# Packed attention and feed-forward on one core: the second-stage matrix P is produced already turned

## The chip, the cores and the metric

The kernel runs on one core of one Trainium2 chip. The metric is device time in microseconds (us) of one execution; lower is better. Engines are named as the profile names them: PE is TensorE's matmul stream, PEld its stream of weight loads, DVE VectorE, ACT ScalarE, POOL GpSimd, SP SyncE (it issues most of the DMAs).

## The reference, cut to what matters

```python
batch, n_heads, seq, head_dim = (8, 8, 576, 64);  n_pack = 32
n_tokens, d_model, d_ff = (4608, 512, 2048)

def sm_attn(qq, kk, vv):
    s = scale * np.matmul(qq, kk.transpose(0, 1, 3, 2))
    s = s - np.max(s, axis=-1, keepdims=True)
    a = np.exp(s)
    a = a / (np.sum(a, axis=-1, keepdims=True) + 1e-09)
    return np.matmul(a, vv)
p_packed = sm_attn(p, k, v)                # 32 packed rows per head: "P"
out = sm_attn(q, p_packed, p_packed)
x = out.transpose(0, 2, 1, 3).reshape(4608, 512)
h = x @ w_in
g = h * (1.0 / (1.0 + np.exp(-1.702 * h)))
return g @ w_out
```

Everything is fp32 outside. The sum of the first softmax runs over the 576 keys; P has, for each of 8 heads, 32 rows of 64 numbers.

## The kernel before, in words

The batches are numbered 0 to 7. Each goes through these steps, one function for each. `scores1` makes the first scores on PE, `scores1_copy` brings them out, `scores1_max` and `bias1` find the maxima, `exp1` takes the exponentials on ACT and adds up their rows, and `sum1` makes half the reciprocal of each sum (`rs1`), a scalar for each of 128 partitions. A partition of these tiles is one packed row of one of four heads; there are two such tiles of 128x576 for a batch, counted by `eo` (0 for even heads, 1 for odd ones). `turn1_blocks` turns 32x32 blocks on DVE, `turn1_out` and `turn1_in` send the blocks through DRAM and back, four stores for each tile and six loads for the batch, and so the weights lie with keys on partitions in `aT`: five groups of 128 keys (`c`), two parities (`e`), 128 columns.

`pack` multiplies them with v. It makes 5 x 2 x 4 = 40 small matmuls, in order of `c`, `e` and the head pair `j`: the stationary side is 128 keys x 32 columns of `aT`, the moving side 128 keys x 64 columns of v, and the four `j` write four strips of 32 partitions. Its result is P, packed rows on partitions, in two PSUM banks (6 and 7). `pack_end` copies the two halves out on ACT, scaled by `rs1`; `pack_turn_mm` turns the 128x128 tile on PE; and `pack_turn_copy` copies the turned tile (`pt`) into SBUF.

`scores2_mm` multiplies `pt` with q into the bank pair `hh`, `scores2_turn` to `turn2` are the second softmax (DVE, POOL, ACT), and `a_upper` / `a_lower` split its weights into two rounded parts. `m_chunk` multiplies `pt` with w_in into M. Then `hp_mm` multiplies M with the second weights (12 matmuls of 288 columns, a pair of feed-forward chunks) into `hh`; `hp_tanh` (ACT) and `hp_gate` (DVE) take the result out of `hh`, which has no second buffer, so `hp_mm` of one pair and `scores2_mm` wait for `hp_gate` of the pair before. `sums_1` to `sums_3`, `g_upper` and `g_lower` prepare its output, and `product` (three matmuls of 256 columns) or `plain` (three of 512) multiply it with w_out into four accumulators `acc`. `take_1` to `take_6` combine those into output rows, `keep` and `keep_over` store them.

The order of all the work is one tuple of 3546 steps, written out by hand or by a planner outside; each engine works through its own instructions in that order, strictly one after the other, and waits are set where data or a buffer ask for it. Steps of attention for one batch stand between the feed-forward steps of the batch ahead of it. Batch 0 goes its own way (`pack_first`, `pack_first_half`, `pack_first_end`), which is the same in both kernels.

Lines of the profile: L184 `warm`, L372 `scores1`, L444 `exp1`, L521 `pack`, L566 `pack_end`, L572 `pack_turn_mm`, L593 `m_chunk`, L627 `scores2_mm`, L635 `scores2_turn`, L702 the gate, L709 `hp_mm`, L759 `out_mm` (the second product of batch 0), L815 `hp_tanh`, L875 `product` and `plain`, L899 to L923 the takes, L934 `keep_over`; L178 and L180 are the copy helper on ACT and on another engine.

Of the kernel before, what the change touches and what calls it, by code (L numbers as in the profile page):

```python
# [24 lines left out]
def kernel(  # L25
# [116 lines left out]
    def bank(i):  # L142
        return pair[0][:, i - 4, :] if pair and i in (4, 5) else banks_all[i]
# [366 lines left out]
    def pn_tile():  # L510
        return words(PN, P).rearrange("p (e d) -> p e d", d=D)

    def pack(b, banks):
        vt = kq["v", b]
        st["bank", "P", b] = [bank(i) for i in banks]
        for c in range(KC):
            for e in range(2):
                t = st["bank", "P", b][e]
                for j in range(NP):
                    e0 = (2 * j + e) * D  # L520
                    nc.tensor.matmul(  # L521
                        t[32 * j : 32 * j + 32, e * D : (e + 1) * D],
                        aT[:, c, e, 32 * j : 32 * j + 32], vt[c][:, e0 : e0 + D],
                        start=(c == 0), stop=(c == KC - 1),
                    )
# [29 lines left out]
    def pack_first_end(b):  # L555
        for eo in range(2):
            t = st["bank", "Pf", 1, eo]
            nc.vector.scalar_tensor_tensor(
                pn_tile()[:, eo, :], t[:, eo * D : (eo + 1) * D], rs1(eo), pf[:, eo, :],
                op0=ALU.mult, op1=ALU.add,  # L560
            )

    def pack_end(b):
        for eo in range(2):
            t = st["bank", "P", b][eo]
            nc.scalar.activation(  # L566
                pn_tile()[:, eo, :], t[:, eo * D : (eo + 1) * D], AF.Copy, scale=rs1(eo)
            )
# [362 lines left out]
    def keep_over(n, i, k, engine=nc.sync):  # L931
# [43 lines left out]
        (m_chunk, 0, 0, (6, 7), 1), (load, 'v', 1, 1), (join_w, 5), (m_upper, 0, 0, 0, 1, act),  # L975
        (h_mm, 0, 1, 1, 5), (m_upper, 0, 0, 1, 1, dve), (upper_w, 5, act), (m_lower, 0, 0, 0, 1),
        (out_mm, 0, 0, 3), (h_tanh, 0, 1, 1), (m_lower, 0, 0, 1, 1), (lower_w, 5, pool),
        (begin_w, 9), (h_gate, 0, 1, 1), (h_mm, 0, 2, 0, 4), (begin_w, 6), (h_mm, 0, 2, 1, 5),
        (join_w, 9), (h_upper, 0, 1, 1, act), (join_w, 6), (h_tanh, 0, 2, 0), (out_mm, 0, 1, 0),
        (begin_w, 7), (h_lower, 0, 1, 1, pool), (out_mm, 0, 1, 1), (h_over, 0, 0, dve),  # L980
        (h_gate, 0, 2, 0), (h_tanh, 0, 2, 1), (h_over, 0, 1, dve), (join_w, 7), (begin_w, 8),
        (h_mm, 0, 3, 1, 4), (over_out, 0), (h_gate, 0, 2, 1), (load, 'v', 1, 0), (begin_w, 11),
        (out_mm, 0, 0, 2), (join_w, 8), (load_w, 13), (begin_w, 10), (out_mm, 0, 1, 2),
        (h_over, 0, 2, dve), (join_w, 11), (load_w, 12), (upper_w, 6, act), (h_mm, 0, 3, 0, 5),
        (join_w, 10), (upper_w, 7, act), (lower_w, 6, pool), (scores1_max, 1, 1),
        (m_chunk, 0, 1, (6, 7), None), (h_tanh, 0, 3, 1), (h_upper, 0, 2, 1, act), (bias1, 1, 1),
        (h_gate, 0, 3, 1), (h_upper, 0, 2, 0, act), (h_lower, 0, 2, 1, pool),
        (m_upper, 0, 1, 1, None, act), (m_upper, 0, 1, 0, None, dve), (out_mm, 0, 1, 3),
        (exp1, 1, 1), (h_lower, 0, 2, 0, pool), (m_lower, 0, 1, 1), (out_mm, 0, 2, 2),
        (m_lower, 0, 1, 0), (h_tanh, 0, 3, 0), (out_mm, 0, 2, 3), (h_upper, 0, 3, 1, act),  # L990
        (turn1_blocks, 1, 1), (h_lower, 0, 3, 1, pool), (h_mm, 0, 6, 0, 4), (turn1_out, 1, 1, 3),
        (h_over, 0, 3, dve), (lower_w, 7, pool), (h_gate, 0, 3, 0), (out_mm, 0, 2, 1),
        (h_tanh, 0, 6, 0), (sum1, 1, 1), (h_upper, 0, 3, 0, act), (load_w, 14), (h_gate, 0, 6, 0),
        (h_mm, 0, 4, 1, 5), (begin_w, 13), (load_w, 15), (scores1_max, 1, 0),
        (h_lower, 0, 3, 0, pool), (begin_w, 12), (h_mm, 0, 4, 0, 4), (bias1, 1, 0), (join_w, 13),
        (out_mm, 0, 3, 2), (join_w, 12), (h_tanh, 0, 4, 0), (turn1_out, 1, 1, 1),
        (h_tanh, 0, 4, 1), (out_mm, 0, 2, 0), (h_upper, 0, 6, 0, dve), (exp1, 1, 0), (load_w, 19),
        (h_lower, 0, 6, 0, dve), (out_mm, 0, 3, 0), (h_gate, 0, 4, 0), (upper_w, 12, act),
        (sum1, 1, 0), (h_gate, 0, 4, 1), (h_mm, 0, 7, 0, 4), (h_upper, 0, 4, 0, act),
        (begin_w, 16), (h_lower, 0, 4, 0, dve), (h_mm, 0, 5, 0, 5), (lower_w, 12, dve),  # L1000
        (h_over, 0, 4, act), (h_tanh, 0, 7, 0), (turn1_out, 1, 1, 2), (join_w, 16),
        (h_upper, 0, 4, 1, act), (out_mm, 0, 3, 1), (begin_w, 14), (load_w, 26),
        (h_lower, 0, 4, 1, pool), (turn1_blocks, 1, 0), (out_mm, 0, 3, 3), (upper_w, 13, act),
        (join_w, 14), (out_mm, 0, 4, 1), (h_tanh, 0, 5, 0), (begin_w, 17), (h_gate, 0, 7, 0),
        (out_mm, 0, 4, 0), (h_gate, 0, 5, 0), (turn1_out, 1, 0, 3), (upper_w, 14, dve),
        (h_upper, 0, 5, 0, act), (out_mm, 0, 4, 3), (join_w, 17), (h_upper, 0, 7, 0, act),
        (load_w, 20), (begin_w, 18), (h_mm, 0, 7, 1, 4), (h_lower, 0, 5, 0, dve),
        (lower_w, 13, dve), (begin_w, 15), (h_mm, 0, 5, 1, 5), (join_w, 18), (join_w, 15),
        (turn1_out, 1, 0, 2), (out_mm, 0, 5, 1), (h_tanh, 0, 5, 1), (begin_w, 19), (load_w, 22),
        (h_gate, 0, 5, 1), (out_mm, 0, 4, 2), (h_upper, 0, 5, 1, act), (join_w, 19),  # L1010
        (h_mm, 0, 6, 1, 5), (begin_w, 20), (lower_w, 14, dve), (h_over, 0, 5, act),
        (m_chunk, 0, 2, (6, 7), None), (h_lower, 0, 5, 1, dve), (turn1_out, 1, 1, 0),
        (upper_w, 15, dve), (h_tanh, 0, 7, 1), (h_lower, 0, 7, 0, dve), (load_w, 23),
        (out_mm, 0, 6, 0), (join_w, 20), (load_w, 21), (h_tanh, 0, 6, 1), (out_mm, 0, 5, 0),
        (h_gate, 0, 7, 1), (lower_w, 15, dve), (h_over, 0, 7, act), (m_upper, 0, 2, 0, None, act),
# [936 lines left out]
```

## Time and profile before

| | us |
|---|---|
| time, median of 3 runs (678.68 to 680.55) | 680.29 |
| time of the profiled execution | 680.52 |
| its span, first to last instruction | 678.7 |
| PE busy | 662.1 (98%) |
| DVE busy | 558.1 (82%) |
| ACT busy | 295.7 (44%) |
| POOL busy | 242.5 (36%) |

A row of the profile gives a line, an engine, an operation, the tiles (out<-in), the shape, a count, then busy time and the mean of one, then the idle time of the engine just ahead of these instructions and what ended it. Matmuls overlap each other in the pipeline, so a record's own length (a few hundred ns) is longer than the distance between two of them; what a stream of matmuls costs is read from the distance of their starts or from busy time over many. The granted TensorE clock was 0.998 of full speed.

### The profile page before, as it was taken

What the parts mean: (1) busy time and instruction counts of PE and PEld (TensorE: products, weight loads), DVE (VectorE), ACT (ScalarE), POOL (GpSimd) and SP (SyncE); (2) the same over time, 40 slices, a digit from 0 to 9 for tenths busy, and PEclk for the clock granted to TensorE, in tenths of its full rate; (3) what the DMA queues carried; (4) which work ended last, traced back from release to release, by engine and by line L of the source; (5) the groups of instructions that cost most, each with busy time, mean ns of one, the idle gap of its engine ahead of it and who ended that gap; (6) DMA issues with size and microseconds to landing.
All of it is one profiled execution on the core that took longest, in us unless ns stands there. A gap on an engine that the chain in (4) does not pass through costs nothing. (4 is left out here: it accounts for less than half of the span.)

```text
span 678.7 us, 15627 instructions
## 1 busy us (share of the span) xinstructions
PE 662.1 (98%) x6037; PEld 593.2 (87%) x6037; DVE 558.1 (82%) x1139; ACT 295.7 (44%) x585; POOL 242.5 (36%) x285
## 2 busy tenths in 40 slices
PE   8999999999999999999999999999999999999996
PEld 6578787897889898998899998899889988999996
DVE  4998788787988899887887778797788878967885
ACT  4787645333453344334534333543344244333231
POOL 2531362331353354323434513333345313442420
PEclk9999999999999999999999999999999999999999
DMA  8997693425562544526543536262445254211032
GB/s 336 417 323 222 226 356 117 111 80 168 171 177 47 149 160 164 137 64 205 197 125 97 127 94 238 88 198 45 154 170 180 57 169 158 82 27 40 11 109 78
DMA packets 94250, 103.11 MB, mean 152 GB/s; under 512 B 69152, under 2 KB 74208, under 8 KB 89568
## 3 DMA queue, kind: packets, MB, share of 16 engines
q1 hardware_dynamic: 94016, 101.86, 47.5%
q8 instruction: 47, 0.77, 0.5%
q10 hardware_dynamic: 160, 0.26, 0.1%
q14 instruction: 27, 0.22, 0.1%
HBM read 80.14 MB, written 21.95 MB: 150 GB/s over the span
## 5 line engine op out<-in xcount | busy, mean ns | idle before, releaser
L875 PE MATMUL acc<-at_float32r 128*128 128x256 f32 (+1 forms) x2553 | 357.6, 291 | 1.2 <-DVE at_float32r L853 0.7
L875 PEld LDWEIGHTS acc<-at_float32r 128*128 128x128 f32 x2553 | 326.6, 188 | 29.1 <-issue 17.4
L709 PE MATMUL hh<-at_float32r 128*128 128x288 f32 x1344 | 206.5, 297 | 2.0 <-DVE at_float L635 1.1
L709 PEld LDWEIGHTS hh<-at_float32r 128*128 128x128 f32 x1344 | 185.4, 188 | 8.4 <-DVE at_float L635 1.9
L178 ACT CAST at_float32r<-at_float 128x512 fp32r<-128x512 f32 (+6 forms) x217 | 120.0, 570 | 100.7 <-PE acc L875 58.1
L815 ACT ACTIVATE at_float<-hh 128x576 f32<-128x576 f32 x112 | 73.1, 653 | 181.1 <-PE hh L709 119.9
L853 DVE TENSOR_TENSOR at_float32r<-at_float,at_float32r 128x512 fp32r<-128x512 f32 (+3 forms) x175 | 116.9, 676 | 18.8 <-ACT at_float32r L178 15.7
L702 DVE SCALAR_TENSOR_TENSOR at_float<-at_float,hh 128x576 f32<-128x576 f32 x112 | 84.2, 752 | 43.5 <-ACT at_float L815 38.6
L853 POOL TENSOR_TENSOR at_float32r<-at_float,at_float32r 128x512 fp32r<-128x512 f32 (+3 forms) x66 | 82.4, 1253 | 100.4 <-DVE at_float32r L180 52.2
L842 POOL TENSOR_TENSOR at_float<-at_float 128x128 f32<-128x128 f32 x55 | 30.2, 551 | 89.2 <-DVE at_float L838 77.1
L180 DVE CAST at_float32r<-at_float 128x416 fp32r<-128x416 f32 (+6 forms) x108 | 47.0, 437 | 8.0 <-POOL at_float L846 3.8
L759 PE MATMUL acc<-at_float32r 128*128 128x512 f32 x192 | 49.4, 396 | 0.0
L608 DVE TENSOR_TENSOR at_float32r<-b,at_float32r 128x512 fp32r<-128x512 f32 (+1 forms) x64 | 42.3, 674 | 2.8 <-ACT at_float32r L178 2.5
L759 PEld LDWEIGHTS acc<-at_float32r 128*128 128x128 f32 x192 | 34.5, 188 | 9.8 <-issue 2.5
L838 DVE TENSOR_TENSOR at_float<-at_float 128x256 f32<-128x256 f32 x80 | 38.6, 485 | 4.9 <-POOL at_float32r L853 1.9
L178 ACT CAST at_float32r<-b 128x512 fp32r<-128x512 f32 (+1 forms) x54 | 30.4, 579 | 25.0 <-PE b L593 24.8
L838 POOL TENSOR_TENSOR at_float<-at_float 128x256 f32<-128x256 f32 x33 | 26.7, 810 | 37.1 <-DVE at_float32r L853 22.0
L846 POOL TENSOR_TENSOR at_float<-at_float 128x128 f32<-128x128 f32 x44 | 24.0, 547 | 40.0 <-DVE at_float L842 38.8
L593 PE MATMUL b<-at_float,at_float 64*32 64x512 f32 (+1 forms) x512 | 34.0, 586 | 0.7 <-DMA at_float<-w_kept 0.7
L709 PEld LDWEIGHTS h<-at_float32r 128*128 128x128 f32 x192 | 27.5, 189 | 5.9 <-DVE at_float L702 1.2
L709 PE MATMUL h<-at_float32r 128*128 128x256 f32 (+1 forms) x192 | 30.3, 300 | 1.0 <-DVE at_float32r L608 0.4
L754 POOL TENSOR_TENSOR at_float32r<-at_float,at_float32r 128x256 fp32r<-128x256 f32 x19 | 16.1, 852 | 38.1 <-ACT at_float32r L178 27.3
(124 smaller groups left out, 532.2 us busy)
## 6 DMA issues: line engine op xcount, KB each, us to landing
at_float<-w_kept SPq DMA_DIRECT2D x24, 1024.0 KB, 5.5
at_float<-v SPq DMA_DIRECT2D x8, 1024.0 KB, 5.7
o<-at_float SPq DMA_DIRECT2D x32, 256.0 KB, 3.0
at_float<-w_out SPq DMA_DIRECT2D x16, 511.8 KB, 6.6
at_float<-q SPq DMA_DIRECT2D x14, 576.0 KB, 5.5
at_float<-w_in SPq DMA_DIRECT2D x12, 511.8 KB, 7.3
at_float<-k_last SPq DMA_DIRECT2D x8, 640.0 KB, 4.9
at_float<-pk SPq DMA_DIRECT2D x8, 576.0 KB, 4.1
```

Source lines behind the costliest of these rows:

```text
L178: nc.scalar.copy(dst, src)
L180: engine.tensor_copy(dst, src)
L593: nc.tensor.matmul(banks[eo][32 * j : 32 * j + 32, columns(part)], pt(b)[rows(eo), j, :], w[rows(eo), j, columns(part)], start=True, stop= ...
L608: nc.vector.tensor_tensor(lo, t[:, at], hi.bitcast(F32), op=ALU.subtract)
L702: nc.vector.scalar_tensor_tensor(dst, th, 1.0, h, op0=ALU.add, op1=ALU.mult)
L709: nc.tensor.matmul(t[:, : halves(b)[half]], m_part(fc, eo, mp)[:, fo : fo + P], a_part(b, half, ap, eo), start=(n == 0), stop=(n == len(te ...
L759: nc.tensor.matmul(acc[i], g0(f, gp)[:, i * P : (i + 1) * P], wo(f, wp), start=(start and n == 0), stop=(stop and n == 2),)
L815: nc.scalar.activation(g, h, AF.Tanh, scale=1.702)
L838: engine.tensor_tensor(dst, src, by, op=ALU.subtract)
L842: engine.tensor_tensor(g_raw(n, p, 6), g_raw(n, p, 5), g_raw(n, p, 1), op=ALU.add)
L853: engine.tensor_tensor(lo, src, g_range(n, p, 0, which)[0].bitcast(F32), op=ALU.subtract)
L875: nc.tensor.matmul(acc[i][:, at : at + m], lhs, rhs, start=(start and k == 0), stop=(stop and k == len(pairs) - 1),)
```

## The change

For batches 1 to 7 the reciprocal is applied to the weights, ahead of the block turn: a new step `norm1` multiplies a 128x576 tile by `rs1` in place, twice a batch (12 times on ACT, 2 times on DVE). `pack_end` and, but for batch 0, `pack_turn_mm` are gone (7 of each). `pack` swaps the sides of its matmuls: v is stationary (128 keys x 64 columns), `aT` moving (128 keys x 32 columns), and the two parities write two strips of 64 partitions of one bank (6). Its result is P turned, and `pack_turn_copy` takes it from there.

```diff
+    def norm1(b, eo, engine=nc.scalar):
+        x = x1(b, eo)
+        if engine is nc.scalar:
+            nc.scalar.activation(x, x, AF.Copy, scale=rs1(eo))
+        else:
+            engine.tensor_scalar(x, x, rs1(eo), None, op0=ALU.mult)
+
-    def pack(b, banks):
+    def pack(b, i):
         vt = kq["v", b]
-        st["bank", "P", b] = [bank(i) for i in banks]
+        st["bank", "PT", b] = t = bank(i)
         for c in range(KC):
-            for e in range(2):
-                t = st["bank", "P", b][e]
-                for j in range(NP):
+            for j in range(NP):
+                for e in range(2):
                     e0 = (2 * j + e) * D
                     nc.tensor.matmul(
-                        t[32 * j : 32 * j + 32, e * D : (e + 1) * D],
-                        aT[:, c, e, 32 * j : 32 * j + 32], vt[c][:, e0 : e0 + D],
-                        start=(c == 0), stop=(c == KC - 1),
+                        t[rows(e), 32 * j : 32 * j + 32], vt[c][:, e0 : e0 + D],
+                        aT[:, c, e, 32 * j : 32 * j + 32], start=(c + j == 0),
+                        stop=(c == KC - 1 and j == NP - 1),
                     )
...
-    def pack_end(b):
-        for eo in range(2):
-            t = st["bank", "P", b][eo]
-            nc.scalar.activation(
-                pn_tile()[:, eo, :], t[:, eo * D : (eo + 1) * D], AF.Copy, scale=rs1(eo)
-            )
...
-        (keep_over, ('over', 1), 1, 1, act), (keep_over, ('over', 1), 0, 1, act),
-        (keep_over, ('over', 1), 0, 0), (keep_over, ('over', 1), 1, 0),
+        (keep_over, ('over', 1), 1, 0), (keep_over, ('over', 1), 1, 1, act),
+        (keep_over, ('over', 1), 0, 0), (keep_over, ('over', 1), 0, 1, act),
```

The table of steps is written anew from its 153rd step on. It holds the same steps but for those named; their places move by up to some tens of steps, and some steps go to another engine: DVE gets 10 more of `g_upper` (86 to 96), 7 more of `g_lower` (175 to 182), 8 more of `h_upper`, 7 more of `norm2`, 10 more of `sums_2`, and gives away 4 of `m_upper`, 4 of `sub2` and 6 of `sums_1`. Three places show it.

On PE, in batch 2, from the end of `pack` to the first `scores2_mm`, before (`at_float_92` is `aT`, `at_float_104` there holds v, later q, and `at_float_232` is `pt`):

```order
L521 MATMUL b_67<-at_float_104,at_float_92 32x64 x4
L521 MATMUL b_68<-at_float_104,at_float_92 32x64 x4
L875 MATMUL acc_65<-at_float32r 128x256 x3
L709 MATMUL hh<-at_float32r 128x288 x12
L875 MATMUL acc_66<-at_float32r 128x512 x6
L875 MATMUL acc_65<-at_float32r 128x512 x6
L709 MATMUL hh<-at_float32r 128x288 x12
L572 MATMUL b_67<-at_float_74,at_float_226 128x128
L875 MATMUL acc_66<-at_float32r 128x512 x3
L875 MATMUL acc_65<-at_float32r 128x512 x3
L627 MATMUL hh<-at_float_104,at_float_232 32x288 x8
```

The same place in the changed kernel, PE again:

```order
L528 MATMUL b_67<-at_float_92,at_float_104 64x32 x40
L709 MATMUL hh<-at_float32r 128x288 x6
L875 MATMUL acc_66<-at_float32r 128x512 x3
L709 MATMUL hh<-at_float32r 128x288 x6
L875 MATMUL acc_66<-at_float32r 128x512 x3
L875 MATMUL acc_65<-at_float32r 128x512 x6
L709 MATMUL hh<-at_float32r 128x288 x12
L875 MATMUL acc_66<-at_float32r 128x512 x9
L627 MATMUL hh<-at_float_104,at_float_232 32x288 x8
```

The pack is now one run of 40 matmuls into one bank, the turn is gone, and between the last `hp_mm` (`128x288 x12`) and `scores2_mm` stand nine matmuls of 512 columns where six and the turn stood.

On ACT, around the first softmax of batch 3, before (`at_float_133` and `at_float_270` are its two tiles of weights):

```order
L178 COPY at_float_270<-hh 128x320
L444 ACTIVATE at_float_133,at_float_89<-at_float_133,at_float_89 128x576
L178 CAST at_float32r<-b_68 128x512
L815 ACTIVATE at_float_350<-hh 128x576
L444 ACTIVATE at_float_270,at_float_89<-at_float_270,at_float_89 128x576
```

The same place in the changed kernel, ACT again:

```order
L444 ACTIVATE at_float_133,at_float_89<-at_float_133,at_float_89 128x576
L178 CAST at_float32r<-at_float_1244 128x256
L516 ACTIVATE at_float_133<-at_float_133,at_float_89 128x576
L815 ACTIVATE at_float_350<-hh 128x576
L178 CAST at_float32r<-at_float_350 128x544
L444 ACTIVATE at_float_270,at_float_89<-at_float_270,at_float_89 128x576
L178 CAST at_float32r<-b_68 128x512
L178 CAST at_float32r<-at_float_1244 128x512
L516 ACTIVATE at_float_270<-at_float_270,at_float_89 128x576
```

Behind each `exp1` (L444) stands now a `norm1` (L516), with one or two other instructions between.

On DVE, at the very end, the takes before:

```order
L902 TENSOR_TENSOR at_float_350<-acc_63,at_float_1429 128x256
L905 TENSOR_TENSOR at_float_1429<-acc_64,at_float_350 128x512
L912 TENSOR_TENSOR at_float_1429<-acc_64,at_float_1429 128x256
L918 TENSOR_TENSOR at_float_1429<-acc_65,at_float_1429 128x512
L923 TENSOR_TENSOR at_float_1429<-acc_66,at_float_1429 128x256
```

The takes in the changed kernel, DVE again:

```order
L902 TENSOR_TENSOR at_float_350<-acc_63,at_float_1474 128x256
L905 TENSOR_TENSOR at_float_1474<-acc_64,at_float_350 128x512
L912 TENSOR_TENSOR at_float_1474<-acc_64,at_float_1474 128x256
L923 TENSOR_TENSOR at_float_1474<-acc_66,at_float_1474 128x256
L918 TENSOR_TENSOR at_float_1474<-acc_65,at_float_1474 128x512
```

The last two takes change places. Behind them ACT issues two of the last four stores and SP two, as before; SP's two change places with each other.

More of the change, by code (lines that the diff above doesn't have):

```diff
@@ L974 @@
         (begin_w, 5), (h_upper, 0, 0, 1, dve), (load_w, 16), (h_lower, 0, 0, 1, pool),
[L975 to L991, printed above, removed]
@@ new lines @@
+        (hp_mm, 3, 4, 0), (g_lower, 3, 2, 0, dve), (plain, 3, 1, 0, 0), (hp_tanh, 3, 4),
+        (plain, 3, 1, 0, 1), (hp_gate, 3, 4), (plain, 3, 2, 0, 0), (hp_over, 3, 4),
+        (both, (scores2_mm, 2, 0, (4, 5)), (m_chunk, 2, 0, (6, 7), None)), (hp_over, 3, 3),
+        (load, 'q', 2, 1), (scores2_turn, 2, 0, 0), (win_in, 2, 1), (plain, 3, 1, 1, 0),
+        (conv_1, 3, dve), (plain, 3, 1, 1, 1), (scores2_turn, 2, 0, 1), (max2, 2, 0),
+        (hp_mm, 3, 5, 1), (g_upper, 3, 3, 0, act), (sub2, 2, 0, None, dve), (hp_mm, 3, 5, 0),
@@ new lines @@
+        (hp_tanh, 3, 6), (a_lower, 2, 0, pool), (plain, 3, 3, 0, 1), (hp_gate, 3, 6),
+        (plain, 3, 3, 1, 1), (hp_over, 3, 6), (g_upper, 3, 5, 0, dve), (conv_4, 4, pool),
+        (both, (scores2_mm, 2, 1, (4, 5)), (m_chunk, 2, 1, (6, 7), None)), (load, 'k', 3, 0),
+        (g_lower, 3, 5, 0, dve), (sums_2, 3, 5, dve), (sums_3, 3, 5, pool),
+        (scores2_turn, 2, 1, 0), (m_upper, 2, 1, 0, None, act), (win_in, 2, 2),
+        (plain, 3, 4, 0, 0), (scores2_turn, 2, 1, 1), (g_upper, 3, 5, 1, act), (plain, 3, 4, 0, 1),
@@ new lines @@
+        (norm1, 3, 0, act), (plain, 4, 0, 1, 0), (bias1, 3, 1), (conv_whole, 2, 1, pool),
+        (turn1_blocks, 3, 0), (hp_mm, 4, 3, 1), (m_upper, 2, 3, 0, None, dve),
+        (turn1_out, 3, 0, 0), (plain, 4, 0, 1, 1), (hp_tanh, 4, 3), (conv_1, 2, dve), (keep, 3, 0),
+        (plain, 4, 1, 0, 0), (conv_2, 2), (g_upper, 4, 2, 0, act), (load, 'v', 3, 1),
+        (hp_gate, 4, 3), (plain, 4, 1, 0, 1), (exp1, 3, 1), (g_lower, 4, 2, 0, dve),
+        (plain, 4, 1, 1, 0), (m_upper, 2, 3, 1, None, act), (sums_1, 4, 3, dve),
@@ new lines @@
+        (a_upper, 5, 1, None, act), (hp_mm, 10, 4, 0), (g_upper, 10, 3, 0, dve),
+        (g_upper, 10, 2, 0, dve), (exp1, 6, 1), (turn1_out, 6, 0, 1), (hp_mm, 10, 4, 1),
+        (g_lower, 10, 2, 0, dve), (g_upper, 10, 2, 1, act), (sum1, 6, 1), (load, 'v', 6, 0),
+        (product, 10, 1, 7), (norm1, 6, 1, dve), (hp_tanh, 10, 4), (product, 10, 1, 5),
+        (product, 10, 1, 6), (sums_1, 10, 3, dve), (product, 10, 1, 3), (hp_gate, 10, 4),
+        (product, 10, 2, 4), (product, 10, 2, 1), (g_lower, 10, 2, 1, dve), (hp_over, 10, 4),
@@ new lines @@
+        (hp_mm, 11, 6, 1), (load, 'k', 7, 0), (sums_3, 11, 4, pool), (sum2, 6, 0),
+        (product, 11, 2, 3), (hp_tanh, 11, 6), (product, 11, 3, 4), (sums_1, 11, 5, pool),
+        (product, 11, 3, 2), (hp_gate, 11, 6), (product, 11, 4, 2), (g_upper, 11, 5, 0, act),
+        (product, 11, 4, 1), (sums_2, 11, 5, dve), (g_lower, 11, 5, 0, dve),
+        (both, (scores2_mm, 6, 1, (4, 5)), (m_chunk, 6, 1, (6, 7), None)), (sums_3, 11, 5, pool),
+        (norm2, 6, 0, None, dve), (g_upper, 11, 4, 1, dve), (scores2_turn, 6, 1, 0),
@@ new lines @@
+        (product, 13, 0, 7), (sums_3, 13, 2, dve), (keep, 12, 1), (g_lower, 13, 1, 1, dve),
+        (hp_mm, 13, 4, 0), (load, 'q', 7, 1), (g_lower, 13, 2, 0, dve), (hp_mm, 13, 4, 1),
+        (sums_1, 13, 3, dve), (sums_2, 13, 3, pool), (product, 13, 0, 6), (hp_tanh, 13, 4),
+        (product, 13, 1, 4), (sums_3, 13, 3, pool), (product, 13, 2, 4), (hp_gate, 13, 4),
+        (product, 13, 1, 2), (product, 13, 2, 2), (product, 13, 0, 5),
+        (both, (scores2_mm, 7, 0, (4, 5)), (m_chunk, 7, 0, (6, 7), None)),
```

1750 lines of the change are left out of this document (863 added, 887 removed).

## The prediction

> **What bounds the kernel now.** I read the busy shares first, then PE's own groups, then one pack in the timeline, then PE's waits, then the end.
>
> ```profile
> PE 662.1 (98%) x6037; PEld 593.2 (87%) x6037; DVE 558.1 (82%) x1139; ACT 295.7 (44%) x585; POOL 242.5 (36%) x285
> 60.00:650.00 590.00, 583.92 (x5374) 530.45 (x5373) 489.63 (x972) 245.58 (x471) 220.23 (x253) 1.00 0.44 135
> ```
>
> The second row is the stretch from 60 to 650 us: span, then busy time of PE, PEld, DVE, ACT, POOL. PE is idle in 6.1 of 590 us there. All seven packs, all turns and all scores of batches 1 to 7 but the first steps of batch 1 lie in it, so an instruction of PE costs its full time, and a step taken from ACT or DVE is worth something only where PE waits for it. What must be priced well is therefore the pack on PE.
>
> ```profile
> L521 PE MATMUL b<-at_float,at_float 128*32 128x64 f32 x560 | 9.3, 220 | 0.0
> L521 PEld LDWEIGHTS b<-at_float,at_float 128*32 128x32 f32 x560 | 8.1, 110 | 1.3 <-issue 1.0
> L875 PEld LDWEIGHTS acc<-at_float32r 128*128 128x128 f32 x2553 | 326.6, 188 | 29.1 <-issue 17.4
> L572 PE MATMUL b<-at_float,at_float 128*128 128x128 f32 x8 | 2.2, 278 | 0.6 <-DVE at_float L558 0.6
> L593 PE MATMUL b<-at_float,at_float 64*32 64x512 f32 x496 | 33.3, 592 | 0.7 <-DMA at_float<-w_kept 0.7
> ```
>
> Of the 40 matmuls of a pack the profile shows 80, since each fp32 matmul runs as two, each with a weight load of its own (560 = 7 x 80). The 128*32 is the part of the array that one takes: four such strips work side by side.
>
> ```profile
> 74.00 1.16 PEld L521 LDWEIGHTS b<-at_float,at_float 128*32 128x32 f32 x80 [0.35 <-issue]
> 74.00 1.32 PE L521 MATMUL b<-at_float,at_float 128*32 128x64 f32 x80
> 75.25 0.97 PE L759 MATMUL acc<-at_float32r 128*128 128x512 f32 x3
> 76.06 0.27 PE L572 MATMUL b<-at_float,at_float 128*128 128x128 f32 x1
> 76.09 0.94 PE L759 MATMUL acc<-at_float32r 128*128 128x512 f32 x3
> 77.47 1.06 PE L593 MATMUL b<-at_float,at_float 64*32 64x512 f32 x16
> ```
>
> This is batch 1's pack and what follows (start, length, engine, line, count). The pack occupies PE from 74.00 until the next stream begins at 75.25.
>
> **The pack, step by step.** Now: 80 instructions on 4 strips are 20 rounds. The run lasts 1.32 us, of which the last record's 0.22 is pipeline, so 19 distances take 1.10, about 56 ns a round with the first load in it. What fills the round is streaming: the 16 matmuls of m_chunk (L593, 512 columns, eight strips, two rounds) last 1.06 us, less the last record's 0.59 and about 0.05 for issuing eight, so 0.42 us for 512 columns, 0.82 ns a column; 64 columns are 52 ns. Loading is hidden: a load of 32 columns is on record with 110 ns, one of 128 columns with 188, so 78 ns for 96 columns, 0.81 ns a column, and 32 columns occupy the loader of a strip for 26 of the 56 ns.
>
> After: v is stationary with 64 columns, so only two strips of 64 fit, 80 instructions are 40 rounds, and the moving side has 32 columns: 32 x 0.82 = 26 ns of streaming. But each instruction loads 64 columns: 64 x 0.81 = 52 ns. The two sides have changed roles and the load is now the longer. Before has no load of 64 columns and no stream of 32, so the round is bounded: below by streaming alone, 26 + 3 = 29 ns (3 being what a round has now over its streaming); above by load and stream one after the other, 52 + 26 + 3 = 81 ns. I take load alone, 52 + 3, about 56 ns, since in the rows of now loads run under the stream of the same strip (26 + 52 would not fit into 56). Forty rounds then last 2.24 us where twenty took 1.12: +1.12 us, and the first load of each pack, which nothing covers, grows by 26 ns. Seven packs: 7 x 1.15 = **+8.0 us** (ends: 7 x (40 x 0.029 - 1.12) = +0.3, and 7 x (40 x 0.081 - 1.12) = +14.8).
>
> The Trainium skill ("TensorEngine Tiling (Array Packing)", Instruction Overhead) says that a matmul with one moving column takes as long as one with 60, and that no tiling should be taken from a dimension that is already small. By it a moving side of 32 streams as long as one of 60, 60 x 0.82 = 49 ns, so a round would be 52 ns whatever the loads do, and the term +6.7 instead of +8.0, an estimate from that page. No row here has a moving side under 64, so the trace neither bears it out nor refutes it.
>
> **The turn.** Seven transposes of 128x128 go.
>
> ```profile
> 152.67 1.55 PE L875 MATMUL acc<-at_float32r 128*128 128x512 f32 x6
> L759 PE MATMUL acc<-at_float32r 128*128 128x512 f32 x192 | 49.4, 396 | 0.0
> ```
>
> Six undisturbed matmuls of 512 take 1.55 us; less a last record of 0.40 that is 0.23 from one to the next. One turn costs PE little: the stream behind starts 0.03 us after it (76.06 to 76.09), and three matmuls of 512 take 0.94 there, about 0.09 more than two distances and a last record (0.86) do undisturbed; 0.12 each, 7 x 0.12 = **-0.8 us** (ends: 0, and 7 x 0.27 = -1.9 with the whole record). Its one wait on record among the seven would have been in the first batch (L558), which stays.
>
> **What the new order gives.** PE's waits ahead of scores2_mm (L627):
>
> ```profile
> PE hh L627 <- DVE at_float32r L180: 0.9, 1, 0.9
> PE hh L627 <- DVE at_float L702: 0.8, 2, 0.7
> PE hh L627 <- DVE at_float L838: 0.5, 1, 0.5
> 157.98 0.48 PE L627 MATMUL hh<-at_float,at_float 64*32 64x288 f32 x8 [0.68 <-DVE at_float L702]
> ```
>
> With 0.2 for q these are 2.4 us, and the last row is batch 2's share: PE stood 0.68 us, because the bank pair hh was still being emptied by the gate. The order puts three more matmuls of 512 (0.69 us) in that place and takes the turn out, 0.57 net, so most of that wait goes. Other batches get between nothing and as much. And since each batch now carries 1.1 us more PE work, DVE and ACT come a little earlier against it. What is late next is the same gate, which DVE reaches behind the work it got from POOL and ACT. I take half of the 2.4 us, **-1.2** (ends: -2.4, and +1.5 if the rewritten table makes as many new waits as the 6.1 us of idle time let me fear).
>
> **Edits with no price.**
>
> ```profile
> L566 ACT ACTIVATE at_float<-b,at_float 128x64 f32<-128x64 f32 x14 | 3.6, 311 | 3.5 <-PE b L521 3.5
> L178 ACT CAST at_float32r<-at_float 128x576 fp32r<-128x576 f32 x11 | 7.4, 675 | 1.8 <-DVE at_float L675 1.6
> L838 DVE TENSOR_TENSOR at_float<-at_float 128x256 f32<-128x256 f32 x80 | 38.6, 485 | 4.9 <-POOL at_float32r L853 1.9
> L853 DVE TENSOR_TENSOR at_float32r<-at_float,at_float32r 128x512 fp32r<-128x512 f32 x79 | 55.2, 700 | 9.1 <-ACT at_float32r L178 7.7
> ```
>
> norm1 has the shape of the 576-wide ACT pass, 0.68 us: 12 on ACT are 8.1 us, and 3.6 of pack_end go, +4.5 on an engine that is busy 44%. On PE's side it hides as long as the chain exp1, norm1, block turn, stores, loads is done before pack; it grows by about 0.7 us for a tile, and in the order the last loads of a batch still stand four to five us of PE work ahead of pack. Shorter by two copies and a turn is the way from pack to scores2_mm, which is priced with the waits above. The stores and loads through DRAM are the same in number and size; in SP's queue they move by a few places, and what is queued behind a store that waits for the later block turn is loads that have those same microseconds. DVE takes over some 25 casts and subtractions at 0.4 to 0.7 us and gives some up; about 14 us more is 84% busy, still below PE, so I price it at nothing and keep it as the likeliest source of new waits.
>
> **The end.**
>
> ```profile
> 670.64 0.37 ACT L899 COPY at_float<-acc 128x256 f32<-128x256 f32 x1 [1.20 <-PE acc L875]
> 672.82 0.69 DVE L918 TENSOR_TENSOR at_float<-acc,at_float 128x512 f32<-128x512 f32 x1
> 673.42 0.42 DVE L923 TENSOR_TENSOR at_float<-acc,at_float 128x256 f32<-128x256 f32 x1
> 673.60 1.20 ACTq L934 DMA_DIRECT2D o<-at_float x2
> 673.87 1.20 SPq L934 DMA_DIRECT2D o<-at_float x2
> ```
>
> From 670.64 DVE works through its takes without a gap, and SP issues its two stores when the last is done. Swapping the last two leaves their sum and SP's two issues; ACT's two issues start with SP's, 0.27 us later than now, and remain beside them. Nothing, at most 0.3 either way.
>
> **The sum.** Against the profiled execution's own 680.52: +8.0 - 0.8 - 1.2 + 0 = +6.0, 686.5. The median shown is 680.29, 0.23 lower, so I forecast 686.3. Its own range, from a round of 50 to 60 ns (+-1.1) and the order's ends (-1.2 to +2.7), with some slack for what was priced at nothing, is 683 to 689.5. A change of 0.3% is 2.0 us, about what can be told from none.
>
> **Rivals.**
>
> The load is hidden, the pack costs as much as now. Then the round is 29 ns, +0.3 - 0.8 - 1.2 = -1.7, 678.6: within 0.3%, and faster by more if the order gives all 2.4 (677.4). For it: loads are fully under streams in every row of now. Against it: in every such row the stream is at least as long as the load (64 against 32 columns, 256 against 128), so hiding was never put to the test. It decides below a round of (1.12 + 2.0 / 7) / 40, about 35 ns. The Trainium skill's page "TensorEngine Tiling (Array Packing)", Theoretical Speedup, counts a factor of two for a stationary side of 64 and four for 32, with no word of loads; by that, half the strips at half the width cost the same.
>
> Load and stream of one strip don't overlap when the load is the longer: 81 ns, +14.8 - 2.0, 693.1. Against it speaks the overlap in the round of now.
>
> The order gives nothing or costs: +8.0 - 0.8 + 1.5, 689.0. PE's idle time is only 6.1 us, and a rewritten table can make as much anew; the cover ahead of scores2_mm, though, grew.
>
> The order gives much more than its waits at scores2_mm, say 5 of the 6.1 us of idle time: 680.29 + 8.0 - 0.8 - 5, about 682.5, just slower or the same. For it: DVE's and ACT's work was moved over the whole span; against it: waits are short and spread over many places.
>
> **Chances.** Load-bound pack with a forecast near mine 0.50, the order giving nothing 0.10, the order giving much more 0.08, hidden load 0.24, load and stream in turn 0.08. The range for eight in ten leaves out the last and the edges of the hidden case: 677.5 to 690. Faster by over 0.3% comes from the better part of the hidden case with a good order: 0.17. The same: the rest of it and half of the generous order, 0.15. Slower: 0.68.
>
> **What would show it.** In the changed kernel's profile the group of the pack's matmuls should have 560 records of 128*64 with 32 columns, about 2.3 us busy for a pack (16 us in all against 9.3), and its weight loads a record near 136 ns (110 + 32 x 0.81). PE busy should rise by about 7. The wait at scores2_mm of batch 2 should be under 0.2. If the pack's run is about 1.3 us, the load was hidden and I am wrong on the main term; if it is 3.3, loads and streams take turns. If the pack is as I say and the time is not, the order is where to look: PE's idle time between 60 and 650 us, against 6.1.

## The result, and the profile after

| | before | changed |
|---|---|---|
| median of 6 runs each | 680.53 us | 686.86 us |
| lowest, highest | 678.68, 681.87 | 686.14, 687.81 |
| profiled execution, its span | 680.52, 678.7 | 686.62, 684.8 |

The ratio is 1.0094 with a 95% interval of 1.0077 to 1.011: 6.4 us slower, 5.2 to 7.5. The forecast was 686.3. Two executions stand far apart and are left out of all ratios: one of the kernel before (2232 us) and one of the variant without `norm1` (1300 us).

The first row is the changed kernel's list of engines (busy us, share of the span, instructions).

```profile
PE 669.6 (98%) x6030; PEld 601.1 (88%) x6030; DVE 563.2 (82%) x1177; ACT 294.3 (43%) x569; POOL 221.2 (32%) x263
```

PE is busy 7.5 us longer than before (662.1). Its idle time over the whole span went from 678.7 - 662.1 = 16.6 to 684.8 - 669.6 = 15.2 us. So 7.5 - 1.4 = 6.1, the growth of the span: all of it is work on PE, and waits gave a little back. The same reading for the stretch from 60 to 650 us (span, then busy PE, PEld, DVE, ACT, POOL):

```profile
60.00:650.00 590.00, 584.64 (x5301) 530.91 (x5300) 489.22 (x993) 240.05 (x448) 197.83 (x230) 1.00 0.44 133
```

PE is idle in 5.4 of 590 us, where it was 6.1. Now the groups of instructions that the change touches (count, then busy time and mean of one, then the idle time ahead):

```profile
L528 PE MATMUL b<-at_float,at_float 128*64 128x32 f32 x560 | 17.7, 223 | 0.0
L528 PEld LDWEIGHTS b<-at_float,at_float 128*64 128x64 f32 x560 | 16.9, 138 | 1.3 <-issue 1.0
L572 PE MATMUL b<-at_float,at_float 128*128 128x128 f32 x1 | 0.3, 329 | 0.6 <-DVE at_float L565 0.6
L516 ACT ACTIVATE at_float<-at_float,at_float 128x576 f32<-128x576 f32 x12 | 9.3, 774 | 2.6 <-DVE at_float L453 2.6
```

The packs took 9.3 us of PE and take 17.7 now, 8.4 more. The weight load's record grew from 110 to 138 ns with its columns, from 32 to 64. One transpose is left, batch 0's. `norm1` is 9.3 us of new work on ACT (0.77 us a pass, where the prediction took 0.68); in batch 2 PE does not wait for it, as the next rows show. They are PE's row of the timeline there, from the pack to the first `scores2_mm` (start, length, engine, line, count):

```profile
149.86 2.52 PE L528 MATMUL b<-at_float,at_float 128*64 128x32 f32 x80
152.31 1.06 PE L709 MATMUL hh<-at_float32r 128*128 128x288 f32 x6
153.22 0.86 PE L875 MATMUL acc<-at_float32r 128*128 128x512 f32 x3
153.92 0.95 PE L709 MATMUL hh<-at_float32r 128*128 128x288 f32 x6
154.71 2.27 PE L875 MATMUL acc<-at_float32r 128*128 128x512 f32 x9
156.81 1.74 PE L709 MATMUL hh<-at_float32r 128*128 128x288 f32 x12
158.39 2.26 PE L875 MATMUL acc<-at_float32r 128*128 128x512 f32 x9
160.58 0.72 PE L627 MATMUL hh<-at_float,at_float 64*32 64x288 f32 x16
```

Three things are to be seen. The pack occupies PE from 149.86 to 152.31, 2.45 us, where before it was 1.25 (74.00 to 75.25). No row carries a bracket with an idle time: the 0.68 us that PE stood ahead of `scores2_mm` are gone. And the pack's own rounds can be read off: the run of 2.52 less the last record's 0.22 are 2.30 us for 39 distances, 59 ns each. Before, 1.10 us for 19 distances were 58 ns. A round costs what it cost, and there are twice as many.

Where PE waits now (total us, times, longest):

```profile
PE hh L709 <- DVE at_float L635: 1.9, 4, 0.8
PE hh L709 <- DVE at_float L702: 1.2, 3, 0.7
PE h L627 <- DMA at_float<-q: 0.6, 1, 0.6
PE hh L627 <- DVE at_float L702: 0.3, 1, 0.3
```

At the `scores2_mm` that write the bank pair `hh` (batches 2 to 7) PE waits 0.3 us in all, where it was 2.4. Batch 1's, which writes the tile `h`, now waits 0.6 us for its q, which it did not before; so of 2.4 us 1.5 are gone. And part has moved: `hp_mm` (L709) waits for the pair `hh` 4.2 us with two smaller rows that are not shown (0.6 for L180, 0.5 for L178), where the like of these came to 2.0 before.

At the end, the takes and the last stores:

```profile
676.91 0.38 ACT L899 COPY at_float<-acc 128x256 f32<-128x256 f32 x1 [1.31 <-PE acc L875]
678.90 0.41 DVE L923 TENSOR_TENSOR at_float<-acc,at_float 128x256 f32<-128x256 f32 x1
679.42 0.69 DVE L918 TENSOR_TENSOR at_float<-acc,at_float 128x512 f32<-128x512 f32 x1
680.18 1.16 SPq L934 DMA_DIRECT2D o<-at_float  x2
```

ACT's copy starts 6.27 us later than before (676.91 against 670.64), and the span is 6.1 longer, so the swapped takes and stores are worth 0.2 us at most.

### The profile page after: what moved, and what is told of

Read it like the earlier page. It is cut to its first block, busy times and chain, and to the rows that moved or that the text cites. A ratio compares the mean times of both kernels' runs of the same rounds, so it can differ in the third digit from the quotient of the medians.

```text
span 684.8 us, 15583 instructions
## 1 busy us (share of the span) xinstructions
PE 669.6 (98%) x6030; PEld 601.1 (88%) x6030; DVE 563.2 (82%) x1177; ACT 294.3 (43%) x569; POOL 221.2 (32%) x263
## 5 line engine op out<-in xcount | busy, mean ns | idle before, releaser
L709 PE MATMUL hh<-at_float32r 128*128 128x288 f32 x1344 | 206.1, 298 | 4.2 <-DVE at_float L635 1.9
L709 PEld LDWEIGHTS hh<-at_float32r 128*128 128x128 f32 x1344 | 185.2, 188 | 11.7 <-DVE at_float L702 3.1
L178 ACT CAST at_float32r<-at_float 128x512 fp32r<-128x512 f32 (+5 forms) x201 | 112.7, 574 | 97.6 <-PE acc L875 55.1
L853 POOL TENSOR_TENSOR at_float32r<-at_float,at_float32r 128x512 fp32r<-128x512 f32 (+3 forms) x59 | 73.4, 1247 | 100.1 <-ACT at_float32r L178 44.3
L838 POOL TENSOR_TENSOR at_float<-at_float 128x256 f32<-128x256 f32 x39 | 30.6, 785 | 89.8 <-DVE at_float L702 45.1
L180 DVE CAST at_float32r<-at_float 128x416 fp32r<-128x416 f32 (+5 forms) x124 | 51.2, 421 | 10.2 <-PE acc L875 5.3
L842 POOL TENSOR_TENSOR at_float<-at_float 128x128 f32<-128x128 f32 x45 | 24.0, 534 | 78.1 <-DVE at_float L838 72.8
L178 ACT CAST at_float32r<-b 128x512 fp32r<-128x512 f32 (+1 forms) x58 | 32.5, 580 | 31.5 <-PE b L593 28.1
L846 POOL TENSOR_TENSOR at_float<-at_float 128x128 f32<-128x128 f32 x41 | 21.4, 523 | 56.4 <-DVE at_float L842 46.9
L838 DVE TENSOR_TENSOR at_float<-at_float 128x256 f32<-128x256 f32 x74 | 35.4, 480 | 1.3 <-POOL at_float32r L853 0.3
L709 PEld LDWEIGHTS h<-at_float32r 128*128 128x128 f32 x192 | 27.6, 189 | 5.2 <-DVE at_float L635 0.8
L709 PE MATMUL h<-at_float32r 128*128 128x256 f32 (+1 forms) x192 | 30.3, 300 | 0.7 <-DVE at_float32r L608 0.4
L846 DVE TENSOR_TENSOR at_float<-at_float 128x128 f32<-128x128 f32 x72 | 24.5, 341 | 4.1 <-POOL at_float L842 3.5
```

What stands on the lines that cost most here:

```text
L178: nc.scalar.copy(dst, src)
L180: engine.tensor_copy(dst, src)
L709: nc.tensor.matmul(t[:, : halves(b)[half]], m_part(fc, eo, mp)[:, fo : fo + P], a_part(b, half, ap, eo), start=(n == 0), stop=(n == len(te ...
L838: engine.tensor_tensor(dst, src, by, op=ALU.subtract)
L846: engine.tensor_tensor(g_raw(n, p, 7), g_raw(n, p, 3), g_raw(n, p, 6), op=ALU.subtract)
L853: engine.tensor_tensor(lo, src, g_range(n, p, 0, which)[0].bitcast(F32), op=ALU.subtract)
```

## The experiments

Ten kernels were run. Ratios are to the kernel before, run beside them on the same chip; where no ratio is given, the kernel ran once, and the time is that one execution's.

**The new order with the old pack.** The table of the changed kernel, without `norm1`; `pack` is the old one (into one bank), `pack_end` stands where the copy stood, turn and copy come one to four of PE's steps later.

```diff
+                        t[32 * j : 32 * j + 32, e * D : (e + 1) * D],
+                        aT[:, c, e, 32 * j : 32 * j + 32], vt[c][:, e0 : e0 + D],
...
+        if s[0] is pack_turn_copy and s[1] > 0:
+            table_of_steps.append((pack_end, s[1]))
...
+                table_of_steps += [(pack_turn_mm, late[1][1], 6), late[1]]
```

> The changed kernel's order with the old pack: norm1 gone, P scaled on the way out (pack_end, where the copy of the turned P stood), turned on PE one to four PE steps later, into one bank; the pack's 40 matmuls have aT stationary (32 columns) and v moving (64). If the pack on PE is the whole price and the new order is worth about what was forecast: pack 9.3 us busy as before, time 686.9 - 8.3 + 0.9 = 679.5 (order worth -1). If the order is worth nothing: 680.5. If the order is itself what costs: 684 or more, though the pack is short.

Measured: 680.98 us (12 runs), ratio 0.9995, 0.9977 to 1.0013. With the pack put back, the loss is gone, and the new order by itself changes nothing that can be told. Its list of engines:

```profile
PE 662.2 (98%) x6037; PEld 592.9 (87%) x6037; DVE 562.0 (83%) x1175; ACT 289.5 (43%) x571; POOL 221.4 (33%) x263
```

PE's idle time is 679.0 - 662.2 = 16.8 us of the span, as before (16.6). Matched with the changed kernel instruction by instruction along PE's stream, each of the seven packs moves what is behind it by 1.15 to 1.21 us, 8.4 in all; the last matmul is only 5.8 us later, so 2.6 are given back between the packs.

**The old order with the new pack.** The table of before; `sum1` and `norm1` stand where the block turn stood, and the block turn just ahead of its first store.

```diff
+        elif s[0] is turn1_blocks:
+            table_of_steps += [(sum1, s[1], s[2]), (norm1, s[1], s[2])]
+            held[s[1], s[2]] = s
+            continue
+        elif s[0] is turn1_out and (s[1], s[2]) in held:
+            table_of_steps.append(held.pop((s[1], s[2])))
```

> The old order with the new pack: norm1 on ACT behind sum1, both put where the block turn stood and the block turn put ahead of its first store; pack swapped, pack_end and pack_turn_mm gone, the copy of P where it stood. If the pack on PE is the price: pack 17.7 us busy, time 680.5 + 8.3 - 0.9 less up to 2 us of waits that the longer pack covers, 686 to 688. If the order of the changed kernel made the loss: 680 to 681.

Measured: 692.91 us (5 runs), ratio 1.017, 1.0148 to 1.0191, five us over what was expected. In the matched streams the packs again take exactly 1.20 us more, seven times; the end is 12.5 later, so some 4 us more than the packs come from something else. What DVE waits for in this kernel:

```profile
DVE at_float L490 <- ACT at_float L516: 6.5, 9, 0.9
```

The block turn (L490) stands still for `norm1`, nine times, 6.5 us. In the kernel before the like was a wait of 0.7 us for `exp1`; in the changed kernel it is 2.5 us, five times. The next two runs take this apart.

**The old order with `norm1` alone.** As the run before, but with the old pack and the turn, and P copied out unscaled, since the weights are scaled already.

```diff
             nc.scalar.activation(
-                pn_tile()[:, eo, :], t[:, eo * D : (eo + 1) * D], AF.Copy, scale=rs1(eo)
+                pn_tile()[:, eo, :], t[:, eo * D : (eo + 1) * D], AF.Copy
             )
```

> The kernel before with norm1 alone, placed as in old_order_new_pack (sum1 and norm1 where the block turn stood, the block turn ahead of its first store), and P copied out unscaled; pack and turn as before. If this placing made the 5 us that old_order_new_pack lost beyond the pack: 680.9 + 4 to 5 = 685 to 686. If they came from the new pack meeting the old order: 681.

Measured: 688.9 us (4 runs), ratio 1.0106, 1.008 to 1.0132: 7.2 us slower (5.5 to 9.0) without a new pack at all, some three more than expected. One of the places, in the timeline:

```profile
371.35 0.78 ACT L516 ACTIVATE at_float<-at_float,at_float 128x576 f32<-128x576 f32 x1
372.16 0.78 DVE L490 STREAM_TRANSPOSE at_float<-at_float 128x576 f32<-128x576 f32 x1 [0.85 <-ACT at_float L516]
373.44 0.74 DVE L709 SCALAR_TENSOR_TENSOR at_float<-at_float,hh 128x576 f32<-128x576 f32 x1
374.23 1.47 PE L716 MATMUL hh<-at_float32r 128*128 128x288 f32 x9 [0.78 <-DVE at_float L709]
```

Read from the bottom: PE stands 0.78 us for the gate (L709 in this kernel), the gate stands in DVE's queue behind the block turn, and the block turn stood 0.85 us for `norm1` on ACT. A wait of DVE becomes a wait of PE of nearly the same size. It is not the only kind: PE's matched stream loses 8.5 us in a dozen places in steps of 0.3 to 1.5, some of them at waits for a transfer.

**The new order without `norm1`.** The changed kernel with its 14 `norm1` left out, so that the weights stay unscaled.

```diff
+    order = tuple(s for s in order if s[0] is not norm1)
```

> The changed kernel without norm1: the weights are left unscaled. If norm1 is hidden in the new order: 686.9, within 0.7. If its 14 passes of 0.7 us hold back the chain or ACT's work for PE: 685 or less.

Measured: 686.95 us, ratio 1.0074, 1.0053 to 1.0095, against the changed kernel's 1.0094, 1.0077 to 1.011. The difference, 1.4 us, is within the two intervals, and in the two profiles it is the stream without `norm1` that ends later, by 0.4 us. In the new order `norm1` is hidden as far as can be told; in the old order, put in roughly, it costs 7 us.

**Loads of 32 columns.** Only the first 32 of each 64 columns of v are made stationary; half of P's rows are not computed.

```diff
-                        t[rows(e), 32 * j : 32 * j + 32], vt[c][:, e0 : e0 + D],
+                        t[e * D : e * D + 32, 32 * j : 32 * j + 32], vt[c][:, e0 : e0 + 32],
```

> The changed kernel with only 32 of v's 64 columns stationary, so half of P's rows are not computed; same 80 instructions on two strips, same 32 moving columns. If the load of the stationary side sets the round: 26 ns of load and 26 of streaming side by side, a round of about 30 ns, pack 1.25 us (9 us busy for seven), time 686.9 - 8 = 678.5. If a narrow moving side takes as long as one of 60 columns: round stays at 52 to 58 ns, pack 17 us busy, 686.9.

Measured: 680.24 us. The number of matmuls, their two strips and the moving side of 32 columns are the changed kernel's; only the load, and with it the width of a strip, is halved. Its batch 1 in the timeline, and the group:

```profile
72.41 1.46 PE L528 MATMUL b<-at_float,at_float 128*32 128x32 f32 x80
```

```profile
L528 PE MATMUL b<-at_float,at_float 128*32 128x32 f32 x560 | 10.2, 197 | 0.1
L528 PEld LDWEIGHTS b<-at_float,at_float 128*32 128x32 f32 x560 | 9.5, 113 | 1.4 <-issue 1.1
```

1.46 less the last record's 0.20 are 1.26 us for 39 distances, 32 ns a round instead of 59. So it is the load that fills the changed kernel's rounds. The time is 1.7 us over what was expected; one execution does not tell that from chance, since the new order with the old pack took 678.8 to 682.9 us beside it. The run also bears on the rule that the prediction had weighed: the Trainium skill ("TensorEngine Tiling (Array Packing)", Instruction Overhead) has a matmul with one moving column last as long as one with 60. The prediction turned these into 60 fp32 columns of 0.82 ns and so into a round of 52 ns, and that estimate fails, for here 32 columns pass in a round of 32 ns. The page itself speaks of about 60 cycles, and a floor below 32 ns was not tested.

**Loads of 128 columns.** One matmul for both parities with 128 stationary columns, half as many matmuls, on a single strip; the weights of one parity are used for both, so that P is not the reference's.

```diff
-                for e in range(2):
...
+                nc.tensor.matmul(
+                    t[:, 32 * j : 32 * j + 32], vt[c][:, 2 * j * D : 2 * (j + 1) * D],
+                    aT[:, c, 0, 32 * j : 32 * j + 32], start=(c + j == 0),
```

> The changed kernel with 128 stationary columns of v and one parity of aT moving, 20 matmuls (40 instructions) for a pack, so P is computed from the even heads' weights alone; 32 moving columns as in the changed kernel. If the load sets the round: 128 x 0.81 = 104 ns and a few, 40 rounds of about 109 ns, 4.4 us a pack, time 686.9 + 7 x 2.0 = 701. If a floor of the moving side sets it: 40 rounds of 52 to 58 ns, no longer than now, 685 to 687.

Measured: 709.19 us. The group and batch 1's pack:

```profile
L526 PE MATMUL b<-at_float,at_float 128*128 128x32 f32 x280 | 34.9, 287 | 0.0
```

```profile
71.53 4.54 PE L526 MATMUL b<-at_float,at_float 128*128 128x32 f32 x40
```

4.54 less the last record's 0.28 are 4.26 us for 39 distances, 109 ns for a load of 128 columns. With 59 for 64 and 32 for 32, a round grows by about 0.8 ns for each further stationary column, which is what the prediction had worked out for a load (0.81). The pack terms add up to 701; the other 8 us are not the pack's rounds at full clock. The granted clock has a mean of 0.982 in this run and 0.999 in the changed kernel's, and 1.7% of 707 us is 12 us of clock, more than enough for the 8. It is told at the end.

**Twice the stream under the same load.** 64 moving columns instead of 32, so that each sum takes in columns that do not belong to it.

```diff
+                    n0 = 64 * (j // 2)
...
-                        t[rows(e), 32 * j : 32 * j + 32], vt[c][:, e0 : e0 + D],
-                        aT[:, c, e, 32 * j : 32 * j + 32], start=(c + j == 0),
+                        t[rows(e), n0 : n0 + 64], vt[c][:, e0 : e0 + D],
+                        aT[:, c, e, n0 : n0 + 64], start=(c + j == 0),
```

> The changed kernel with 64 columns moving instead of 32 (two heads' weights at once, so P holds sums of wrong products), 64 stationary, 80 instructions on two strips. If the longer of load and stream sets the round: both 52, round stays 58 ns, 686.9. If a round is the load plus a part of the stream: up to 84 ns, +1.0 us a pack, 694.

Measured: 687.19 us, and in batch 1:

```profile
71.88 2.55 PE L529 MATMUL b<-at_float,at_float 128*64 128x64 f32 x80
```

2.55 - 0.22 = 2.33 us, where 32 moving columns took 2.30. Doubling the stream costs 0.03 us a pack: it lies under the load. Load and stream of one strip overlap with the stream longer (before: 52 ns of stream, 26 of load, a round of 58), with the load longer (the changed kernel, 59) and with both alike (here, 60).

**The same pack on four strips.** Each matmul is split into two with 32 stationary columns, so that four strips are in use.

```diff
+                    for d0 in (0, 32):
+                        e0 = (2 * j + e) * D + d0
+                        at = e * D + d0
...
+                            t[at : at + 32, 32 * j : 32 * j + 32], vt[c][:, e0 : e0 + 32],
```

> The changed kernel with each pack matmul cut in two along v's 64 columns: 32 stationary, 32 moving, 80 matmuls (160 instructions) on four strips; same result. If a round lasts as long as the longer of load and stream and strips work side by side: rounds of 32 ns as with 32 columns on two strips, 40 of them, a pack of 1.3 us where the changed kernel has 2.3, 10 us busy for seven, time 686.9 - 7 x 1.0 = 679.8. If 160 instructions with their loads are bound by their issue (7 ns each, load and matmul in turn): 160 x 13 = 2.1 us a pack, time 685.5.

Measured: 685.89 us, ratio 1.0068, 1.0045 to 1.0092. The interval overlaps the changed kernel's (1.0077 to 1.011), so it is not shown to be better, and it is far from the 679.8 that the load alone would give. Two of its packs in the timeline, batch 3's and batch 4's:

```profile
230.36 1.46 PE L530 MATMUL b<-at_float,at_float 128*32 128x32 f32 x134
232.86 0.44 PE L530 MATMUL b<-at_float,at_float 128*32 128x32 f32 x26 [1.04 <-issue]
...
308.76 1.63 PE L530 MATMUL b<-at_float,at_float 128*32 128x32 f32 x160
```

Batch 4's is close to what was expected (1.3), 1.43 us from first to last start against the changed kernel's 2.30. Batch 3's has a hole after its 134th instruction, in which PE waits for nothing that the profile shows. Three of the seven packs have one: 0.38 us after 126 instructions (batch 2), 1.24 after 134 (batch 3), 1.18 after 146 (batch 7), 2.8 us in all. In these three a packet of a queue that carries instructions had begun within a microsecond of the pack's start; in the other four none had (the nearest began 1.4 to 1.7 us away).

The holes are not all that ate the gain. The profiled execution took 688.2 us, over the median, and PE stood idle 21.1 us of it, where the changed kernel's has 15.2. Two rows at `scores2_mm` (L629 in this kernel) together weigh more than the holes:

```profile
PE h L629 <- DMA at_float<-q: 1.6, 1, 1.6
PE hh L629 <- DVE at_float L704: 1.6, 1, 1.6
```

They are 3.2 us where the changed kernel has 0.9. Short packs alone don't bring them: the kernel with loads of 32 columns, whose packs are as short, has 0.8 there. What does is not shown.

**Four strips, in two pieces.** The same pack cut into 96 and 64 instructions, with one step of PE between the pieces where there is one ahead of the copy.

```diff
+        for c in {None: range(KC), 0: range(3), 1: range(3, KC)}[part]:
...
+        if late is not None and s[0] in (plain, product, hp_mm, out_mm):
+            cut_order.append((*late, 1))
+            late = None
```

> The four-strip pack of the run before, cut into two pieces of 96 and 64 instructions, with a PE step of 6 to 12 matmuls between the pieces in batches 2 to 7 (batch 1 has none to put there, its two pieces stay together). Same work, same rounds of 31 ns. If the holes inside three of the packs come from instructions that do not arrive as fast as 160 short ones in a row are consumed, the pieces are short enough and the holes of batches 2 to 7 go: 683 to 684, and no gap over 0.3 us inside a pack. If they come from something else in those places (a transfer, a semaphore), they stay: 685.5 to 687.

Measured: 687.43 us, ratio 1.0082, 1.0053 to 1.0111. Only in batches 2 and 6 was there a step to put between; the other five packs remained whole. So the run tells less than was meant. Batch 3's pack:

```profile
229.74 1.47 PE L532 MATMUL b<-at_float,at_float 128*32 128x32 f32 x134
231.81 0.44 PE L532 MATMUL b<-at_float,at_float 128*32 128x32 f32 x26 [0.60 <-issue]
```

The two uncut packs that had a long hole have it again, behind the very same instruction, the 134th and the 146th (0.80 and 1.13 us between starts); the cut pack that had one, batch 2's, has none. In batches 2, 3 and 7 a packet of the instruction queue again began within 1.2 us of the pack's start. That speaks for a place in the program, not for a transfer's chance, and fits instructions that arrive more slowly than 160 short ones in a row are used up. It is not shown: one pack lost its hole, and that was the smallest. The cut also made a wait of its own, 0.27 us at the `hp_mm` between the pieces, and the time did not get better.

**The old order without the turn.** The kernel before, with the old pack (into one bank) and without `pack_end` and the seven turns; the copy takes the pack's tile as it is, so P is unscaled and unturned.

```diff
+    order = tuple(
+        s for s in order if s[0] is not pack_end and not (s[0] is pack_turn_mm and s[1] > 0)
+    )
```

> The kernel before, in its own order, with the old pack (into one bank) and without pack_end and the turn on PE in batches 1 to 7: the small copy takes the pack's unscaled, unturned tile straight on as pt (so P is left unscaled and unturned; the work behind it is the same in kind). If a turn costs PE only its place in the stream, 7 x 0.12 = 0.8 us go: 679.7, within 0.3% of before. If the way pack, copy, turn, copy is what scores2_mm and m_chunk wait for, a microsecond or two of their waits goes as well: 677.5 to 678.5.

Measured: 681.23 us, ratio 0.9997, 0.9979 to 1.0014. PE is busy 0.7 us less:

```profile
PE 661.4 (97%) x6030; PEld 592.4 (87%) x6030; DVE 558.9 (82%) x1139; ACT 292.0 (43%) x571; POOL 242.2 (36%) x285
```

The waits took it back; the largest of PE's:

```profile
PE hh L626 <- DMA at_float<-q: 3.2, 3, 1.6
```

`scores2_mm` (L626 here) waits 3.2 us for its q, where before it was 0.2. A turn is worth its 0.1 us of PE, and a shorter way past it brought `scores2_mm` nothing: in this execution q is what is late. Why q comes later here is not shown.

## Why the prediction was right, point by point

The time came out at 686.86 (forecast 686.3), slower as forecast, and by the mechanism that was forecast.

| term | forecast | measured |
|---|---|---|
| pack, seven | +8.0 | +8.4 |
| turn, seven | -0.8 | -0.7 to -0.8 |
| waits (order) | -1.2 | -1.2 in idle time of PE up to its last matmul |
| norm1, ACT, DVE | 0 | 0 in this order |
| end | 0 | -0.2 |
| sum, span | +6.0 | +6.1 |

The pack is the term that the runs show. That the waits match to a tenth is luck, as told below.

**The pack.** "I take load alone, 52 + 3, about 56 ns" was the step on which all hung. Three sizes of load and two of stream bear it out: 32, 59 and 109 ns for 32, 64 and 128 columns, and no change when the stream is doubled. Both ends of its bound fall: a hidden load (29 ns a round) and load and stream in turn (81 ns). The term was 0.4 short, because 39 distances of 59 ns against 19 of 58 make 1.20 us for a pack, against 1.15. Part of that was in the rows of before: 1.10 us over 19 distances are 58 ns, not the 56 that the prediction wrote, so a round had 6 ns over its streaming and not 3, and 52 + 6 would have been 58. The weight load's record was put at 136 ns and is 138. The packs' busy time was put at 16 us and is 17.7: seven times the pack's run of 2.52, whose last record reaches into the next stream; the prediction had left that record out.

**The turn.** In the trace of before the instruction after a turn starts 26 to 28 ns behind it, and the next one comes 82 to 86 ns later than it does elsewhere (314 against 230 ns for 512 columns): 0.11 us a turn where 0.12 was taken. PE's busy time without the turns is 0.7 lower. But taken out alone it moved the time by nothing that can be told.

**The order.** Half of 2.4 us was a guess between two ends. PE's idle time up to its last matmul did fall by 1.2 (10.96 to 9.74), but the sources were only partly those named. At `scores2_mm` 1.5 of the 2.4 us went, batch 2's 0.68 wholly, as said. "What is late next is the same gate" was right too: `hp_mm` waits 2.2 us more for the pair `hh`, which more than takes that back. The rest is small waits in other places, 0.7 for a weight part and 0.7 ahead of `product` among them, which are gone. And the size is not shown to be the order's. The new order with the old pack has no less idle time than before (16.8 us of the whole span, against 16.6), and its time is the same within -1.6 to +0.9 us. Longer packs, which give the other engines more time, don't explain the fall either: without `norm1` the new order has the same long packs and 16.8 us idle, and with loads of 32 columns it has short packs and 15.4, near the changed kernel's 15.2. Part of these differences is waiting for transfers (0.8 us for k and 0.3 for the turned weights in the one without `norm1`). A single profile therefore does not tell a term of -1.2 from nothing, and the match is luck.

**The edits with no price.** DVE's busy time rose by 5.1 us where about 14 was feared, and ACT's fell by 1.4 where +4.5 was reckoned, since ACT gave away casts. `norm1` was said to hide as long as the chain ahead of pack is done before it. It does hide in the new order, as far as can be told. Yet the danger was in another place than the chain: in DVE's queue, where the block turn waits for `norm1` and the gate stands behind the block turn. Put roughly into the old order, it cost 7.2 us, nearly as much as the packs. So the price of zero was right because the rewritten table has a place for it; the prediction took the table for a term of its own and did not see that it makes room for `norm1`. In the changed kernel the rest of that wait is 2.5 us of DVE, and PE shows none of it by name.

**The rivals.** The hidden load and the load in turn with the stream are refuted on the chip. The good order did not come: nothing gave 5 us. The rival that the order costs 1.5 stays nearest to what the order alone did, and its 689.0 is above every run of the changed kernel.

What stays open: of the 2.6 us that came back between the packs, what each wait gave beside the turns' 0.8; and whether the old pack could gain anything from a better order, since none of the versions run here was faster than the kernel before by more than can be told.

## What to carry to other kernels

Before the sides of a small fp32 matmul are swapped, count the columns that each side sends: the round of a strip was here the longer of load and stream and about 6 ns, and narrowing the stream gains nothing once the load is the longer, while a wider stationary side halves the strips that work side by side. On an engine that is busy 98% a saved transpose is worth its distance in the stream (0.11 us here), not its record (0.28). A step that is put on a half idle engine costs what its follower's queue holds back: look at what stands behind the waiting instruction before pricing it at zero.

## What the runs showed of the hardware that was not expected

**The clock fell under a run of loads.** In the kernel with loads of 128 columns the mean granted clock was 0.98. Below are windows of two us in batch 3 (span, busy PE, PEld, DVE, ACT, POOL, then the granted clock, DMA share, GB/s):

```profile
231.00:233.00 2.00, 2.00 (x20) 2.00 (x19) 1.93 (x5) 0.65 (x1) 0.46 (x1) 1.00 0.10 16
233.00:235.00 2.00, 2.00 (x19) 2.00 (x18) 2.00 (x3) 0.00 (x0) 1.26 (x1) 0.89 0.30 41
235.00:237.00 2.00, 2.00 (x11) 2.00 (x11) 0.98 (x2) 0.00 (x0) 0.58 (x1) 0.50 0.71 253
```

PE and its loads are busy without a gap, and yet the clock goes to half, some three microseconds into the pack (it starts at 231.52), and a round from 112 to 213 ns. It did so inside three of the seven packs, and a fourth time 0.7 us behind batch 4's. The trace's record of the clock has the four falls at 234.57, 319.90, 418.89 and 500.81 us, for 6.8, 3.4, 6.8 and 6.8 us; half clock for 23.9 us is the 12 us of clock. The falls lie 25, 29 and 24 times 3.413 us apart, so they look like decisions taken at fixed steps of 3.413 us. In the step that ended at each fall the pack had run for 79 to 100% of the time; in the three packs without a fall it ran for at most 76% of any step. That may be why only some packs were hit. The Trainium skill ("TensorE: Matmul & The Clock Gate", Part 1: The HAM clock gate) ties the fall of the clock to a window of idleness; here PE shows none. That streaming, not loading, is what counts as activity would explain it (a round streams for some 26 of 112 ns), and was not tried.

**Short matmuls follow each other closely.** In the changed kernel's packs two matmuls on different strips start 6 to 7 ns apart, and with loads of 32 columns 32 moving columns pass in a round of 32 ns. The holes in three of the packs of 160 instructions are the only thing seen here that may be a limit on issue.
